# Start of a fused convolution and gated feed-forward kernel: the first input moved to other queues, and one mask cleared by another engine

## The chip, the cores and the metric

The kernel runs on one core of a Trainium2 chip. The metric is the device time of one execution in microseconds (us); lower is better. A core has five engines that run their own instruction streams: PE (TensorE, matrix products), DVE (VectorE), ACT (ScalarE), POOL (GpSimd) and SP (SyncE, which here only issues transfers). Transfers (DMAs) can be issued from SP, ACT and POOL, and all of them are moved by the same 16 DMA engines. Only a DMA that POOL issues changes the type on the way (float32 in memory to float16 on the chip); one from SP or ACT copies bytes.

## The reference

The input x is 8 sequences of 4096 tokens with 192 channels. A causal convolution over 7 tokens comes first, with one set of softmaxed weights per head (8 heads of 24 channels); after it a gated feed-forward layer.

```python
w = softmax(weight, axis=-1)                       # weight is [8 heads, 7 taps]
x_pad = concatenate([zeros(B, 6, D), x], axis=1)
out[b, s, h, g] = sum_k w[h, k] * x_pad[b, s + k, h, g]
t = out.reshape(B * S, D)                          # 32768 x 192
y = (maximum(t @ w_gate, 0) * (t @ w_val)) @ w_out # 192 -> 1536 -> 192
```

## The kernel before, in words

Two sequences are worked on at a time, as two "streams" (`st` 0 and 1, batch entries 0 and 4 at the start). They lie side by side in the partitions: 64 channels of stream 0 in partitions 0 to 63, the same channels of stream 1 in partitions 64 to 127. The work is cut into 16 units of 1024 tokens (`NUNIT`), each of two windows of 512 tokens. For each unit, `gate_val` multiplies the convolved input `xc` by `Wg` and `Wv` (PE, L505), ACT takes the positive part (L516), DVE multiplies the two (L517), and `project` multiplies by `Wo` (PE, L539, or L559 for the first unit). From unit 2 on the convolution itself is done by ACT, DVE and POOL beside the products. Units 0 and 1 are convolved on PE, with banded matrices: for unit 0 `conv_dense` (L333) multiplies 110 tokens of x by a 110 x 104 band per head.

The order on every engine is the order in which the program is written (`manual_schedule`). Everything that the change touches lies before the first product. Three things must be there before the first matmul of L333:

- The band matrices. `wr` (the weights) comes by SP (L104). DVE takes the maximum (`mx`, L214), ACT the exponential (`ex`, L217), DVE the sum, its reciprocal and `over` (L224). A matmul (L235) spreads them over 112 rows, DVE makes `diag` (L245), 14 matmuls with `places` (L255) spread that over the band, and DVE copies the first band out of PSUM (L288, `fill_band(0, [0, 1, 2], ...)`). `places`, `same` and `over` are made from `spaced`, a mask that is cleared (L129) and then gets its ones from POOL's `affine_select` (L131). ACT's first instruction is the load of its function table (L148), which comes with a small throwaway activation, `spare`.
- Stream 0's x. The first window is cut into five token steps of 104 tokens (`jj` 0 to 4). SP brings steps 1 to 4 in float32 into `stage`, an area in the tile `prods` (L125), and ACT casts them to float16 into `xts[0]`, the tile `x_h` (L279). Step 0 of both streams needs zeros ahead of the sequence: DVE clears the place (L140), SP brings it (L141), DVE casts it (L294).
- Stream 1's x, steps 1 to 4: POOL brings it, cast on the way, straight into `x_h` (L130).

For the first 64 channels L333 takes steps 1 to 4 of stream 0 first (16 matmuls), then steps 1 to 4 of stream 1 (16), then step 0 of both (8); the other two channel blocks of 64 follow with 40 matmuls each. Until then PE runs products of constants (`warm_up`, L157): seven at the start, one after L235, two after L255.

POOL's queue at the start is: clear `spaced` (L129), issue stream 1's x (L130), `affine_select` (L131), and then the issues of the weight slices `Wg` and `Wv` (L173) and of the next x (L90). DVE copies the first weight slice to the other 64 partitions (L180) before the first product with it.

Of the kernel before, what the change touches and what calls it, by code (L numbers as in the profile page):

```python
# [15 lines left out]
def kernel(  # L16
# [12 lines left out]
    nc = tc.nc  # L29

    B, S, D = x.shape
# [3 lines left out]
    PAD = KW - 1  # L35
    NB = B // 2
# [5 lines left out]
    SUB = 112  # L42
# [4 lines left out]
    GSUB = 5  # L47
    DSUB = 104
# [49 lines left out]
    xts = {}  # L98
    ROWS0 = DSUB + PAD
# [7 lines left out]
    def stage(p0, rows, st, n_st, jj, n):  # L107
        at = room[p0 : p0 + rows, 0, 0, 0:1]
        dims = [[D * GSUB, n_st], [D, n], [1, D]]
        return bass.AP(  # L110
            tensor=at.tensor,
            offset=at.offset + D * (GSUB * st + jj),
            ap=[at.ap[0]] + [d for d in dims if d[1] > 1],
        )

    xts[0] = xpool.tile([128, GSUB, 2, D], F16, name="x_h")

    def body(st):
        return bass.AP(
            tensor=x.tensor,  # L120
            offset=x.offset + (NB * st * S + DSUB - PAD) * D,
            ap=[[D, SUB], [DSUB * D, GSUB - 1], [1, D]],
        )

    nc.sync.dma_start(out=stage(0, SUB, 0, 1, 1, GSUB - 1), in_=body(0))  # L125
    ones = const.tile([128, SUB], FP)
    nc.vector.memset(ones[:], 1.0)
    spaced = const.tile([SUB, KW, SEG + 2 * GAP], FP)
    nc.gpsimd.memset(spaced[:], 0.0)  # L129
    nc.gpsimd.dma_start(out=xts[0][0:SUB, 1:GSUB, 1, :], in_=body(1))  # L130
    nc.gpsimd.affine_select(  # L131
        out=spaced[:, :, GAP : GAP + SEG],
        in_=ones[0:SUB, 0 : KW * SEG].rearrange("p (k s) -> p k s", k=KW),
# [8 lines left out]
        out=stage(PAD, DSUB, 0, 2, 0, 1),  # L142
        in_=bass.AP(
            tensor=x.tensor, offset=x.offset, ap=[[D, DSUB], [NB * S * D, 2], [1, D]]
        ),
# [53 lines left out]
    def summed(out, step, n, at):  # L199
# [15 lines left out]
        out=mx[:], in_=wr[:], axis=mybir.AxisListType.X, op=ALU.max, negate=True  # L215
# [9 lines left out]
        out=over[:],  # L225
# [10 lines left out]
        out=spread[0:SUB, 0, 0:H],  # L236
# [7 lines left out]
    with nc.allow_low_precision("products with one and zero"):  # L244
        nc.vector.tensor_tensor(  # L245
            out=diag[:],
# [6 lines left out]
    for a in range(2):  # L253
        for b in range(NSEG):
            nc.tensor.matmul(  # L255
                out=(bps, spread)[a][:, a, HB * SEG * b : HB * SEG * (b + 1)],
# [12 lines left out]
    for h in range(H):  # L269
        r = G * h  # L270
        while r < G * (h + 1):
            c, n = r // 64, min(64 - r % 64, G * (h + 1) - r)
            nc.sync.dma_start(
                out=tap[r % 64 : r % 64 + n, c, :],
                in_=taps[h : h + 1, :].unsqueeze(1).to_broadcast([1, n, KW]),
            )
            r += n

    nc.scalar.copy(out=xts[0][0:ROWS0, 1:GSUB, 0, :], in_=stage(0, ROWS0, 0, 1, 1, GSUB - 1))  # L279
    bands = {}  # L280

    def fill_band(a, heads, copy):
# [431 lines left out]
```

## Time and profile before

| what | value |
|---|---|
| median of 3 runs | 768.64 us (768.06 to 768.94) |
| span of the profiled execution, first to last instruction | 767.4 us |
| median less that span | 1.24 us |
| PE busy | 761.4 us, 99% of the span |
| DVE, ACT, POOL busy | 692.2, 601.7, 369.9 us |
| granted TensorE clock | 1.000 |

The profile shows one execution. Its own time has no row beside its span; the 1.24 us by which the median of the runs is longer is what lies around the span. Busy shares are averages over the whole span: PE at 99% is busy from about 6.5 us to the end, and what it lacks is in the first 6.5 us. Times in a timeline are counted from the start of the span. In a row of a timeline the first number is the start, the second the duration (of a group, from its first start to its last end), then engine, line, operation and operands; a bracket at the end gives the idle time before it and what ended it. "SPq", "ACTq" and POOL's DMA rows are the issuing of a transfer and not the transfer.

### The profile page before, as it was taken

How to read it: one execution, taken by the hardware profiler on the slowest of the kernel's cores; microseconds unless marked ns; L12 is line 12 of the kernel's file. 1: busy time of each engine (PE TensorE's matmuls, PEld its weight loads, DVE VectorE, ACT ScalarE, POOL GpSimd, SP SyncE). 2: the span in 40 equal slices, each digit the busy share in tenths (PEclk: the TensorE clock that was granted, in tenths of full speed). 3: DMA queues.
4: the chain of work that ended last, by engine and by line, in shares of the span. 5: the costliest groups of instructions: out<-in, count | busy, mean ns of one | idle time of the engine just before them, and what ended most of it. 6: DMA issues, size and time to landing. Idle time of an engine off the chain costs nothing.

```text
span 767.4 us, 24881 instructions
## 1 busy us (share of the span) xinstructions
PE 761.4 (99%) x10842; PEld 502.1 (65%) x10842; DVE 692.2 (90%) x745; ACT 601.7 (78%) x736; POOL 369.9 (48%) x212
## 2 busy tenths in 40 slices
PE   9999999999999999999999999999999999999997
PEld 4495674946649476584855848567494674947657
DVE  7999999999999999999999999999999999995590
ACT  6797887878888788888878878788787887874671
POOL 8608648093570926619165290843809355080000
PEclk9999999999999999999999999999999999999999
DMA  8956727180462705428064271722719131200202
GB/s 121 138 97 118 91 90 88 54 122 6 100 78 69 107 23 98 59 85 94 26 112 43 85 91 44 109 28 89 89 50 110 21 95 37 65 21 23 63 2 85
DMA packets 131827, 56.13 MB, mean 73 GB/s; under 512 B 96757, under 2 KB 131717, under 8 KB 131717
## 3 DMA queue, kind: packets, MB, share of 16 engines
q1 hardware_dynamic: 90805, 38.85, 24.9%
q0 software_dynamic: 40768, 15.59, 18.8%
q8 instruction: 85, 1.39, 0.8%
q14 instruction: 25, 0.20, 0.1%
q10 hardware_dynamic: 144, 0.10, 0.0%
HBM read 31.68 MB, written 25.17 MB: 74 GB/s over the span
## 4 chain that ended last, share of the span: by engine, by line
PE 99%; DMA 1%; issue 0%; DVE 0%; POOL 0%; POOLq 0%
PE ps L505 65%; PE ps L539 31%; PE ps L559 2%; DMA x_h<-in_x_dram 1%; PE ps L333 0%; PE ps L358 0%; DVE acc L576 0%; POOL spaced L129 0%; POOLq L698 0%
## 5 line engine op out<-in xcount | busy, mean ns | idle before, releaser
L517 DVE TENSOR_TENSOR hT<-gr,ps 128x1024 f16<-128x1024 f16 (+1 forms) x386 | 469.0, 1216 | 36.9 <-ACT gr L516 9.9
L516 ACT ACTIVATE gr<-ps 128x1024 f16<-128x1024 f32 (+1 forms) x386 | 393.3, 1020 | 101.9 <-PE ps L505 100.1
L458 POOL TENSOR_TENSOR prods<-prods 128x1344 f32<-128x1344 f32 x70 | 212.5, 3035 | 309.8 <-DVE prods L454 306.4
L505 PE MATMUL ps<-xc,Wg 64*128 64x512 f16 x2304 | 311.9, 376 | 0.0
L505 PE MATMUL ps<-xc,Wv 64*128 64x512 f16 x2304 | 311.8, 376 | 0.0
L539 PEld LDWEIGHTS <-hT 64*128 64x128 f16 x5760 | 238.0, 94 | 3.6
L539 PE MATMUL ps<-Wo,hT 64*128 64x192 f16 x5760 | 240.1, 243 | 0.0
L505 PEld LDWEIGHTS <-Wv 64*128 64x128 f16 x2304 | 129.6, 94 | 118.7 <-DVE hT L517 0.3
L505 PEld LDWEIGHTS <-Wg 64*128 64x128 f16 x2304 | 112.2, 94 | 132.5 <-issue 0.5
L481 DVE SCALAR_TENSOR_TENSOR acc<-x_r,tap,acc 128x576 f32<-128x576 f16 x210 | 154.3, 815 | 1.6 <-DMA x_r<-x_p 1.6
L452 ACT ACTIVATE prods<-x_r,tap 128x448 f32<-128x448 f16 x222 | 130.4, 664 | 0.0
L576 ACT COPY out_s<-ps 128x768 f32<-128x768 f32 (+1 forms) x64 | 46.2, 722 | 53.9 <-PE ps L539 44.0
L414 POOL DMA_DIRECT2D x_e<-in_x_dram x56 | 45.2, 818 | 3.3 <-POOL x_p L433 3.3
L433 POOL COPY x_p<-x_e 128x1728 f16<-128x1728 f16 x28 | 44.8, 1627 | 1.5 <-DMA x_e<-in_x_dram 1.5
L458 POOL TENSOR_TENSOR xc<-prods 128x1344 f16<-128x1344 f32 x14 | 42.4, 3026 | 1.1
L481 DVE SCALAR_TENSOR_TENSOR xc<-x_r,tap,acc 128x576 f16<-128x576 f16 x42 | 31.8, 816 | 0.0
L469 ACT ACTIVATE acc<-x_r,tap 128x576 f32<-128x576 f16 x42 | 29.4, 768 | 0.0
L454 DVE TENSOR_SCALAR prods<-x_r,tap 128x448 f32<-128x448 f16 x72 | 27.4, 452 | 0.0
L576 DVE COPY out_s<-ps 128x384 f32<-128x384 f32 x14 | 7.8, 556 | 14.8 <-ACT out_s L576 14.8
L559 PE MATMUL ps<-Wo,hT 128*128 128x192 f16 x192 | 16.2, 246 | 0.0
L559 PEld LDWEIGHTS <-hT 128*128 128x128 f16 x192 | 15.9, 98 | 0.0
L576 DVE COPY acc<-ps 128x192 f32<-128x192 f32 x1 | 0.4, 358 | 14.2 <-PE ps L539 14.2
(52 smaller groups left out, 62.6 us busy)
## 6 DMA issues: line engine op xcount, KB each, us to landing
out_dram<-out_s SPq DMA_DIRECT2D x62, 384.0 KB
x_e<-in_x_dram POOLq DMA_DIRECT2D x34, 192.0 KB, 6.2
x_e<-in_x_dram POOLq DMA_DIRECT2D x22, 240.0 KB, 5.0
x_r<-x_p SPq DMA_TRANSPOSE x126
Wo<-in_moe_w_out_dram POOLq DMA_DIRECT2D x1, 576.0 KB
x_h<-in_x_dram POOLq DMA_DIRECT2D x2, 240.0 KB, 7.3
x_h<-in_x_dram POOLq DMA_DIRECT2D x2, 210.0 KB, 4.7
x_h<-in_x_dram POOLq DMA_DIRECT2D x2, 192.0 KB, 7.7
```

The costliest lines, as they stand in the source:

```text
L414: nc.gpsimd.dma_start(out=xe[:, j : j + n, st, :, :].rearrange("p j c r -> p j (c r)"), in_=bass.AP(tensor=x.tensor, offset=x.offset + (b ...
L433: nc.gpsimd.tensor_copy(out=xp[:, :, :, st, :], in_=xe[:, :, st, :, :])
L452: engine.activation(out=out, in_=in_, func=ACTF.Copy, scale=scale)
L458: nc.gpsimd.tensor_tensor(out=pr[:, 0] if k < KW - 1 else xc[u][:, :, LDVE:UNIT], in0=pr[:, 0], in1=pr[:, k], op=ALU.add,)
L469: nc.scalar.activation(out=accs[u][:, c, :], in_=shifted(u, c, 0, 0), func=ACTF.Copy, scale=tap[:, c, 0:1],)
L481: nc.vector.scalar_tensor_tensor(out=xc[u][:, c, 0:LDVE] if k == KW - 1 else acc[:, c, :], in0=shifted(u, c, k, 0), scalar=tap[:, c, k : k ...
L505: nc.tensor.matmul(out=pss[i][:, st, :], lhsT=W[64 * st : 64 * st + 64, c, 128 * f : 128 * (f + 1)], rhs=xcb[64 * st : 64 * st + 64, c, WI ...
L516: nc.scalar.activation(out=gr[:, sts], in_=pss[0][:, sts], func=ACTF.Relu)
L517: nc.vector.tensor_tensor(out=h[:, f, sts], in0=gr[:, sts], in1=pss[1][:, sts], op=ALU.mult)
L539: mm = nc.tensor.matmul(out=outs[q], lhsT=h[64 * r : 64 * r + 64, f, st, 128 * q : 128 * (q + 1)], rhs=Wo[64 * r : 64 * r + 64, f, :], sta ...
L559: nc.tensor.matmul(out=outs[q], lhsT=h[:, f, st, 128 * q : 128 * (q + 1)], rhs=Wo[:, f, :], start=(f == 0), stop=(f == NFF - 1),)
L576: one(out=dst[:, step * j : step * j + step], in_=src[:, step * j : step * j + step])
```

## The change

Three edits, all ahead of the first product.

- POOL's first instruction becomes the issue of stream 1's x. It stood behind the clearing of `spaced`, which DVE does now, second in its queue, between `ones` and the clearing of the place for step 0.
- Stream 0's x, steps 1 to 4, is brought in two transfers: steps 1 and 2 from ACT's queue, steps 3 and 4 from SP's. Each has half the bytes.
- ACT casts the two halves with two instructions instead of one.

```diff
-    def body(st):
+    def body(st, jj, n):
         return bass.AP(
             tensor=x.tensor,
-            offset=x.offset + (NB * st * S + DSUB - PAD) * D,
-            ap=[[D, SUB], [DSUB * D, GSUB - 1], [1, D]],
+            offset=x.offset + (NB * st * S + DSUB * jj - PAD) * D,
+            ap=[[D, SUB], [DSUB * D, n], [1, D]],
         )
 
-    nc.sync.dma_start(out=stage(0, SUB, 0, 1, 1, GSUB - 1), in_=body(0))
+    nc.gpsimd.dma_start(out=xts[0][0:SUB, 1:GSUB, 1, :], in_=body(1, 1, GSUB - 1))
+    nc.scalar.dma_start(out=stage(0, SUB, 0, 1, 1, 2), in_=body(0, 1, 2))
+    nc.sync.dma_start(out=stage(0, SUB, 0, 1, 3, 2), in_=body(0, 3, 2))
     ones = const.tile([128, SUB], FP)
     nc.vector.memset(ones[:], 1.0)
     spaced = const.tile([SUB, KW, SEG + 2 * GAP], FP)
-    nc.gpsimd.memset(spaced[:], 0.0)
-    nc.gpsimd.dma_start(out=xts[0][0:SUB, 1:GSUB, 1, :], in_=body(1))
+    nc.vector.memset(spaced[:], 0.0)
     nc.gpsimd.affine_select(
...
-    nc.scalar.copy(out=xts[0][0:ROWS0, 1:GSUB, 0, :], in_=stage(0, ROWS0, 0, 1, 1, GSUB - 1))
+    for jj in (1, 3):
+        nc.scalar.copy(
+            out=xts[0][0:ROWS0, jj : jj + 2, 0, :], in_=stage(0, ROWS0, 0, 1, jj, 2)
+        )
```

In the built program each engine's list keeps its order but for these places: POOL begins with the issue of stream 1's x; DVE has the clearing of `spaced` second; ACT begins with the issue of its half, and the load of its function table (L148) comes behind that; SP has the same number of transfers, the second one of half the size. PE's list is the same.

## The prediction

> **What bounds the kernel now.** I read the page's busy shares first, then the chain of waits for the first 9 us, then the timeline of those 9 us, then the row of transfers that resemble the moved one.
>
> ```profile
> PE 761.4 (99%) x10842; PEld 502.1 (65%) x10842; DVE 692.2 (90%) x745; ACT 601.7 (78%) x736; POOL 369.9 (48%) x212
> ```
>
> PE is the bound: it lacks 6 us of the span. After 6.55 the chain of waits holds nothing but PE, so an edit at the start is worth exactly the time by which PE's unbroken run begins earlier or later. The chain up to there:
>
> ```profile
> 0.82 0.33 POOL spaced L129
> 1.16 0.28 issue
> 1.43 5.08 DMA x_h<-in_x_dram
> 6.51 0.04 issue
> 6.55 1.60 PE ps L333 x103
> 8.15 6.71 PE ps L505 x60
> ```
>
> Stream 1's x is what arrives last: POOL clears the mask (0.33), idles 0.28, issues at 1.43, and 5.08 later the data is there. What is next behind it is in the timeline:
>
> ```profile
> 0.82 1.28 ACT L148 ACT_TABLE_LOAD   x1 [0.82 <-PEq L698]
> 0.83 0.40 SPq L104 DMA_DIRECT2D wr<-in_weight_dram  x1
> 0.92 0.15 DVE L127 MEMSET ones<- 128x112 f32 x1 [0.92 <-PEq L698]
> 1.09 0.38 DVE L140 MEMSET prods<- 32x384 f32 x1
> 1.29 0.34 SPq L125 DMA_DIRECT2D prods<-in_x_dram  x1
> 1.68 0.46 SPq L141 DMA_DIRECT2D prods<-in_x_dram  x1
> 2.19 0.15 DVE L214 TENSOR_REDUCE mx<-wr 8x1 f32<-8x7 f32 x1 [0.46 <-DMA wr<-in_weight_dram]
> 2.37 0.39 ACT L217 ACTIVATE ex<-wr,mx 8x112 f32<-8x112 f32 x1
> 4.86 0.51 DVE L288 CAST band<-ps 128x336 f16<-128x336 f32 x1 [0.45 <-PE ps L255]
> 5.05 0.83 ACT L279 CAST x_h<-prods 110x768 f16<-110x768 f32 x1 [1.53 <-DMA prods<-in_x_dram]
> 5.93 2.22 PE L333 MATMUL ps<-band,x_h 110*32 110x104 f16 x120 [0.64 <-ACT x_h L279]
> 6.55 1.45 PEld L333 LDWEIGHTS <-x_h 110*32 110x32 f16 x104 [0.23 <-DMA x_h<-in_x_dram]
> ```
>
> Three arrivals in a row: the first band at 5.37 (4.86 + 0.51), stream 0's x cast at 5.88 (5.05 + 0.83), stream 1's x at 6.51. PE does stream 0's 16 matmuls from 5.93 to about 6.24 (their weight loads are 0.02 apart, so 0.31 for 16), and then waits until 6.55. Take the last arrival away and the next stands 0.3 behind it; the third 0.5 behind that.
>
> **The change part by part, as a sum over the three arrivals.**
>
> Stream 1's x. The issue loses the 0.33 of clearing ahead of it. Whether the 0.28 of idling goes too, the trace does not show: SP's first issue begins at 0.83 without a gap, which gives an issue at 0.82; if the gap belongs to every first issue it is 1.10. I take 0.95, nearer to SP's row. The 5.08 to landing I keep, because it is mostly the transfer's own:
>
> ```profile
> x_e<-in_x_dram POOLq DMA_DIRECT2D x22, 240.0 KB, 5.0
> ```
>
> Transfers of its kind, some of them with the DMA engines free at the time, need 5.0. So it lands at 6.03 (5.90 to 6.18) instead of 6.51, and PE can use it 0.04 later, at 6.07 (5.94 to 6.22).
>
> Stream 0's x. ACT issues its half at 0.82 instead of SP at 1.29, SP the other half at 1.29. The whole transfer needed 3.76 from issue to cast (1.29 to 5.05); half of it needs no more, so the halves land by 4.58 and 5.05 at the latest. A cast of 768 elements took 0.83 and one of 448 0.53 (L288 on ACT), so 384 take 0.46: the second half is cast by 5.51 at the latest, against 5.88. The extra cast costs 0.10 of ACT, beside the wait for data that ACT has anyway (1.53 before L279).
>
> The band. Here is the price. ACT's issue stands ahead of its table load, behind which `spare`, `ex` and the whole band chain are queued, and SP's tap transfers and the matmul of L235 wait for that chain. At the end of the trace there is one issue by ACT:
>
> ```profile
> 763.44 0.39 ACTq L577 DMA_DIRECT2D out_dram<-acc  x1
> ```
>
> SP's are 0.34 to 0.46. With 0.39 the table load ends at 2.49 instead of 2.10, `spare` (0.20) at 2.71, and `ex` starts at 2.76 instead of 2.37. Before, it waited for `mx` (ready 2.34) and `spare` (2.32) at once, so it has no slack, and the links to the band (sum, reciprocal, `over`, L235, `diag`, L255, copy) follow each other with gaps under 0.2. So the band comes at 5.76 instead of 5.37. The bounds are 0 (if the issue runs beside the load) and 0.46, SP's longest.
>
> The mask. DVE does 280 elements in about 0.31 (between 112 in 0.15 and 384 in 0.38), ready at 1.40. POOL comes to `affine_select` 0.33 to 0.61 earlier than 2.38, at 1.77 or later, so it waits for nothing; `over` needs it at about 3.6. On DVE the mask pushes `prods`, `places` and `ex`'s clearing 0.31 later, to about 2.05, still ahead of `mx`, which waits for `wr` until 2.19: nothing. But the clearing of `prods` ends at 1.78, so SP's step 0 (L141) is issued at 1.98, 0.3 later. With its old 4.09 it lands at 6.07 at the latest and is cast by 6.43, when PE has just finished stream 1's 16 matmuls (6.43): free, barely; it also has less ahead of it in SP's queue (half of L125). If that cover goes it costs up to 0.1, because band 3 and the weight copies stand behind the cast on DVE.
>
> POOL's other issues (`Wg`, `Wv`, next x) move 0.3 to 0.6 earlier with the first, so the weights, which DVE waited for until 6.91, come ahead of the need, and PE's steps after 8.15 move as a block.
>
> Sum: stream 0 can start when the band is there, 5.76 + 0.05 = 5.81; its 16 matmuls end at 6.12; stream 1 is there at 6.07. PE goes on at 6.12 instead of 6.55: 0.4 (0.33 to 0.43 over the bounds of the issue). The span becomes 767.0, and with the 1.24 around it the median 768.64 becomes 768.2.
>
> At one place a rule lowers that. In the window 3.2 to 3.4 the trace has 95 packets of the hardware queue and none of POOL's; POOL's began at 3.9, and from 4.4 to 4.6 there were 37 and 41. Moved earlier, POOL's packets meet more of SP's. The Trainium skill ("DMA: Bandwidth & Descriptors", Queues, rings and completion order) says that each DMA engine takes turns between its queues packet by packet; the window from 4.4 to 4.6 agrees. By that rule stream 1's x would land later than 6.03 by about the 0.2 that a share of the remaining packets takes (my estimate), and the gain would be 0.3 instead of 0.4.
>
> **The rivals.**
>
> No gain: POOL's first issue has a start of its own, or its transfer waits for SP's packets, and stream 1's x still lands at about 6.5. For: packets of POOL came only 2.5 after its issue, while for `x_e` (issue at 19.59) it was 1.6, so 0.9 of the 5.08 may be a fixed start. Against: 5.0 is the usual time. Time 768.6.
>
> More gain: ACT's issue does not hold up the table load. Then stream 0 starts at 5.51 + 0.05 and stream 1's x sets the time, at 5.94: 0.6, time 768.0.
>
> A late table: ACT's first issue costs more than SP's. PE starts stream 1 at 5.42 + d + 0.31, with d the delay of the table, so the change loses only if d is over 0.82. POOL's issue took 0.88, but ACT's and SP's were half of it. With d = 1.2 the time is 769.0.
>
> The other side, a slow PE: the seven constant products at the start end at 3.69, and L235 follows at 3.62 without a gap. With `ex` 0.39 later L235 starts at 4.01, and PE idles about 0.3. The first 512-column products are 0.425 apart (1.25, 1.67, 2.10, 2.53); the half-array pairs of L505 later are 0.215 apart, and the change of rate falls between 3.4 and 4.0, just where the new gap comes. If the gap puts the full rate off, all of L333 runs at half of it: 1.6 more for the 104 matmuls, 0.3 for stream 0's, 0.2 for L255, less 0.4: +1.7, 770.3. It takes the full rate to come after about 9.8; if it comes at 7, the loss is about 0.8 and the net +0.4. Against it: the work on PE is the same, and the gap of 0.64 ahead of 5.93 did not slow what follows and now shrinks to about 0.1. The Trainium skill ("TensorE: Matmul & The Clock Gate", Part 1) has the rule behind it: the PE clock is doubled only after a busy window of about 3.4 us, and the windows run freely. The profile's granted clock is 1.00 in all of these windows, so it cannot show this; the spacing of the matmuls can.
>
> **How the numbers follow.** Forecast 0.55; more gain 0.08; no gain 0.15; late table 0.08; slow PE 0.10; 0.04 is left for a gain that nothing in the profile shows. About 0.2% (1.5 us) is what a measurement of this kernel can tell from no change, and all cases but slow PE and the remainder lie within it, with 0.01 of the late table beyond: faster 0.04, same 0.85, slower 0.11. The range goes from the better case (768.0) to the late table (769.0), widened at each end by most of the 0.44 between the ends and the middle of the runs: 767.6 to 769.3.
>
> **What would show it.** Right: POOL's issue at 0.8 to 1.1, `x_h` landing near 6.0, ACT's table load at about 1.2 and `ex` at 2.76, the first band's copy ending at 5.76, L333's first matmul at 5.8 released by DVE's band and not by ACT's cast, and the unbroken run of PE from about 6.1. Wrong: `ex` still at 2.4 (more gain), `x_h` at 6.5 (no gain), 512-column products 0.43 apart after 4.0 or L333 taking over 2.5 (slow PE), or a chain of waits that leaves PE after 9 us.

## The result

The changed kernel is slower: 770.37 us in the median of 9 runs (769.49 to 771.00) against 768.54 us of the kernel before (9 runs, 767.70 to 768.94). The ratio is 1.0020, with an interval of 1.0012 to 1.0029. The forecast was 768.2 with a range of 767.6 to 769.3. In two further sessions, each on one chip, the ratio was 1.0025 (1.0015 to 1.0035) and 1.0015 (1.0006 to 1.0024).

The profiled execution of the changed kernel has a span of 768.2 us. Its chain of waits for the first 12 us no longer contains the landing of stream 1's x; it runs from ACT's issue through the band matrices (start, duration, engine and operation):

```profile
0.83 0.40 ACTq L126
...
2.75 0.29 ACT ex L218
...
4.07 0.51 PE ps L236 x2
4.58 0.54 PE ps L158
5.12 0.75 PE ps L256 x14
5.87 0.53 PE ps L158 x2
6.40 3.01 PE ps L337 x100
```

L337 is L333 of before. The chain begins to count it a little after its start: all 120 of its matmuls take 3.08 us (in the timeline below), 0.026 each, where the last 103 of before took 1.60, 0.0155 each. From then on PE is busy without a break in both kernels, so the 1.26 us by which it enters the products later (9.41 against 8.15) stay to the end of PE's work, at 763.06 before (754.81 + 8.25) and 764.33 after (759.79 + 4.54):

```profile
754.81 8.25 PE L539 MATMUL ps<-Wo,hT 64*128 64x192 f16 x196
759.79 4.54 PE L543 MATMUL ps<-Wo,hT 64*128 64x192 f16 x106
```

In the 20 profiles of this case PE ends 754.8 to 755.2 us behind the end of L333, wherever that lies. The spans of these two executions differ by 0.8 only. Behind PE's end, the last of the output landed after 3.0 us before and after 2.0 in the changed kernel, which is scatter (2.0 in 17 of the 20 profiles), and from that landing to the end of the span it took 1.3 before and 1.8 after, which is not; "The end of the program" below comes back to it.

What lies around the span was taken as 1.24 us ahead of the prediction. That was the median of the runs less the span of another execution. Where time and span of one execution are on record, the difference is 1.65 to 3.47 us over 153 executions of the kernel before (median 1.74) and 1.69 to 2.74 over 30 of the changed kernel (median 1.99). So one execution's time says little about a change of 1 us, and the span says more.

The timeline of the changed kernel's profile shows why PE enters the products later:

```profile
0.83 0.40 ACTq L126 DMA_DIRECT2D prods<-in_x_dram  x1
0.86 2.83 PE L158 MATMUL ps<-const-bfloat16-1.0 128*128 128x512 bf16 x7 [0.86 <-PEq L702]
1.26 1.28 ACT L149 ACT_TABLE_LOAD   x1 [1.26 <-PEq L702]
1.40 0.88 POOL L125 DMA_DIRECT2D x_h<-in_x_dram  x1 [0.87 <-POOLq L702]
2.66 0.37 ACT L218 ACTIVATE ex<-wr,mx 8x112 f32<-8x112 f32 x1
3.71 0.91 ACT L281 CAST x_h<-prods 110x384 f16<-110x384 f32 x2
4.07 0.51 PE L236 MATMUL ps<-over,ex 8*112 8x8 f32 x2 [0.38 <-DVE same L202]
4.51 0.61 PE L158 MATMUL ps<-const-bfloat16-1.0 128*128 128x512 bf16 x1
5.53 0.51 DVE L292 CAST band<-ps 128x336 f16<-128x336 f32 x1 [0.63 <-PE ps L256]
6.33 3.08 PE L337 MATMUL ps<-band,x_h 110*32 110x104 f16 x120
9.34 0.50 PE L509 MATMUL ps<-xc,Wg 64*128 64x512 f16 x2
9.68 0.38 PE L509 MATMUL ps<-xc,Wv 64*128 64x512 f16 x2
```

Three things are to be seen. POOL's issue did not move: it begins at 1.40 instead of 1.43, with 0.87 of idling ahead of it. The table load stands behind ACT's issue, the exponential comes at 2.66 instead of 2.37, and PE idles 0.38 ahead of L236. And the single 512-column product that follows takes 0.61; in the profile of before it took 0.39:

```profile
4.01 0.39 PE L157 MATMUL ps<-const-bfloat16-1.0 128*128 128x512 bf16 x1
```

This product is the gauge for the rest: 0.61 is PE at half rate, 0.39 at full rate. (Half, because such products start 0.425 apart in the first group and the pairs of L505 later 0.215 apart; a single duration and the pace of L333 change by less.) In the changed kernel the full rate comes only between 9.34 (0.50) and 9.68 (0.38); before, it came by 4.01. The granted clock column stays at 1.00 all the while and shows nothing of it.

### The profile page after: what moved, and what is told of

Same layout as the page of the kernel before. It is cut to its first block, busy times and chain, and to the rows that moved or that the text cites. A ratio compares the mean times of both kernels' runs of the same rounds, so it can differ in the third digit from the quotient of the medians.

```text
span 768.2 us, 24882 instructions
## 1 busy us (share of the span) xinstructions
PE 763.1 (99%) x10842; PEld 508.7 (66%) x10842; DVE 692.9 (90%) x746; ACT 601.2 (78%) x737; POOL 369.8 (48%) x211
## 3 DMA queue, kind: packets, MB, share of 16 engines
q8 instruction: 84, 1.38, 0.8%
## 4 chain that ended last, share of the span: by engine, by line
PE 99%; ACT 0%; DVE 0%; issue 0%; ACTq 0%; DVEq 0%
PE ps L509 65%; PE ps L543 31%; PE ps L563 2%; PE ps L337 1%; PE ps L362 0%; PE ps L158 0%; ACT L149 0%; PE ps L256 0%; PE ps L236 0%; DVE over L225 0%; ACTq L126 0%; DVE acc L580 0%; ACT ex L218 0%; ACT spare L149 0%; DVE sm L222 0%
## 5 line engine op out<-in xcount | busy, mean ns | idle before, releaser
L509 PEld LDWEIGHTS <-Wv 64*128 64x128 f16 x2304 | 131.6, 94 | 116.9 <-DVE hT L521 0.3
L509 PEld LDWEIGHTS <-Wg 64*128 64x128 f16 x2304 | 115.2, 94 | 129.3 <-issue 0.5
```

The costliest lines, as they stand in the source:

```text
L509: nc.tensor.matmul(out=pss[i][:, st, :], lhsT=W[64 * st : 64 * st + 64, c, 128 * f : 128 * (f + 1)], rhs=xcb[64 * st : 64 * st + 64, c, WI ...
```

## The experiments

Each time below is a median, beside that of the kernel before on the same chip; the ratio of the two has a 95% interval. "Rate at" is where the profile of that kernel changes from half to full rate, read from the 512-column products and the pace of L333 (about 0.025 a matmul at half rate, 0.0155 at full).

**Which part costs.** The split of stream 0's x alone, and POOL's part alone (issue first, mask on DVE):

```diff
+    nc.scalar.dma_start(out=stage(0, SUB, 0, 1, 1, 2), in_=body(0, 1, 2))      # split alone
+    nc.sync.dma_start(out=stage(0, SUB, 0, 1, 3, 2), in_=body(0, 3, 2))
-    nc.sync.dma_start(out=stage(0, SUB, 0, 1, 1, GSUB - 1), in_=body(0))
...
+    nc.gpsimd.dma_start(out=xts[0][0:SUB, 1:GSUB, 1, :], in_=body(1))          # POOL's part alone
...
-    nc.gpsimd.memset(spaced[:], 0.0)
-    nc.gpsimd.dma_start(out=xts[0][0:SUB, 1:GSUB, 1, :], in_=body(1))
+    nc.vector.memset(spaced[:], 0.0)
```

> The kernel before with the split of stream 0's x alone (half from ACT, half from SP, two casts); POOL's order and the mask as before. ACT's issue delays the table load and with it the exponential by 0.3. Theory A: the whole loss is here, 769.9 to 770.7, with L337 at half rate. Rival (the loss comes from POOL's and DVE's part): 768.3 to 768.8.

> The kernel before with POOL's part alone: the issue of stream 1's x first on POOL, the mask cleared by DVE; stream 0's x in one transfer from SP. Theory A (ACT's issue is what costs, and POOL's first issue begins at about 1.40 whatever stands ahead of it): the same as before, 768.2 to 768.8, x landing at 6.5 to 6.6, first PE product of L333 at 5.9. Rival (the later zero of step 0 or the mask on DVE cost something): 769 or more. Rival (POOL's issue does move here): 768.1 and an issue before 1.2.

The split: 770.16 against 768.76, ratio 1.0016 (1.0007 to 1.0025), nearly the whole loss, with the idle 0.39 on PE and the rate at about 8.9. Stream 1's x landed 4.9 us after its issue there, no later than before (5.1). POOL's part: 768.26, ratio 0.9991 (0.9982 to 0.9999). A repeat of POOL's part gave 768.74 against 768.32, 1.0001 (0.9990 to 1.0011), so neither a gain nor a loss is shown.

> POOL's part of the change alone, a second time. If it is a gain: 0.998 to 0.9995 of the kernel before. If the first session was scatter: 0.9995 to 1.0005. POOL's issue at 1.40 in both cases, so nothing of the forecast's earlier landing is expected.

Four lines of the first of the two profiles:

```profile
1.41 0.88 POOL L125 DMA_DIRECT2D x_h<-in_x_dram  x1 [0.87 <-POOLq L698]
4.09 0.61 PE L157 MATMUL ps<-const-bfloat16-1.0 128*128 128x512 bf16 x1
5.25 0.66 PE L157 MATMUL ps<-const-bfloat16-1.0 128*128 128x512 bf16 x2
5.88 1.96 PE L333 MATMUL ps<-band,x_h 110*32 110x104 f16 x120
```

POOL's first issue stays at 1.41 with nothing ahead of it. And PE is at half rate at 4.09 although nothing on PE's side differs from the kernel before: the rate changed at about 5.6 in this execution, and the time was good all the same.

**Does the idle time of PE do it?** One more constant product in the changed kernel closes the gap ahead of L236; one fewer opens a gap of 0.36 in the kernel before; and without the whole first group PE idles from the start to 3.64.

```diff
-    warm_up(512, 512, 512, 512, 512, 512, 128)
+    warm_up(512, 512, 512, 512, 512, 512, 512, 128)   # changed kernel, filled
+    warm_up(512, 512, 512, 512, 512, 128)             # kernel before, with a gap
...
-    warm_up(512, 512, 512, 512, 512, 512, 128)        # kernel before, no first group
```

> The changed kernel with one more 512-column constant product in the first warm-up group, so that PE is busy until about 4.1 us instead of 3.69, when the matmul of L236 starts at 4.07. Theory A (the idle 0.38 us of PE ahead of L236 puts the full rate off, and half-rate products up to 9.4 are the loss): full rate comes at about 4 again, the 120 matmuls of L337 take about 2.2 us instead of 3.1, PE's unbroken run starts where stream 1's x lands (6.6, as before), and the time is that of the kernel before, 768.2 to 768.8. Theory B (the loss is the later band chain and the queues themselves, the rate is an effect of the profile): nothing changes, 770.0 to 770.8. Theory C (the rate changes at random times in each execution, whatever PE did before): the spread stays and the middle lies anywhere between 768.5 and 770.4.

> The kernel before with one 512-column constant product fewer in the first warm-up group: nothing else is moved, PE just idles about 0.36 us from 3.26 to 3.62. Theory A (the idle time ahead of L235 puts the full rate off): L333 takes about 3 us, the time rises by 1.2 to 2.0 to 769.8 to 770.6. Theory B (it was the band chain and the queues): 768.3 to 768.8, no change. Theory C (random): no change of the middle beyond 0.3.

> The kernel before without the first group of seven constant products: PE idles until L235 at 3.62 instead of being busy from 0.86. Windows theory: a spoiled window costs the same whether 0.4 or 2.8 us in it are idle, and the full rate comes 3.4 to 6.8 after the first steady work; the loss is bounded by half rate for all of L333 (0.8 of PE's start, the rest being hidden by the wait for stream 1's x) and a part of the first products: 769.3 to 771. Rival (the rate depends on the amount of idle time): eight times the idle time of the kernel with one product fewer, and some 3 to 5 us, 772 or more.

Filled: 769.02 against 768.76, 1.0004 (0.9995 to 1.0012), rate at about 4.3, a little over the 768.2 to 768.8 that was expected. Its profile, an execution of 769.25 us, has no idle time ahead of L236 but a wait of L337 for stream 1's x:

```profile
4.51 0.39 PE L158 MATMUL ps<-const-bfloat16-1.0 128*128 128x512 bf16 x1
6.88 1.55 PE L337 MATMUL ps<-band,x_h 110*32 110x104 f16 x104 [0.43 <-DMA x_h<-in_x_dram]
```

With the gap: 769.31 against 768.76, 1.0005 (0.9996 to 1.0013), below the 769.8 to 770.6 of theory A. The profile has the rate at about 9.5:

```profile
3.62 0.51 PE L235 MATMUL ps<-over,ex 8*112 8x8 f32 x2 [0.36 <-ACT taps L267]
5.88 3.08 PE L333 MATMUL ps<-band,x_h 110*32 110x104 f16 x120
8.89 0.61 PE L505 MATMUL ps<-xc,Wg 64*128 64x512 f16 x2
```

Without the group: 769.29 against 768.28, 1.0006 (0.9997 to 1.0014). By these times neither of the two is told apart from no loss; the spans further down do tell them apart, with a loss that is smaller than the change's. It hardly grows with the idle time (0.36 or 2.8 us). In these two kernels the band is on time, L333 starts at 5.9, and at half rate it runs through the time in which it would have waited for stream 1's x. In the profile with the gap the first product starts at 8.89 against 8.09, 0.8 later and not 1.3.

**Is the place of the rate's change fixed?** The kernel before and the changed kernel, once more:

> The kernel before once more, for a second profile of the same program. If the place of the window differs from execution to execution, the change of rate (512-column products 0.61 long before it, 0.39 after it, in the first 10 us) need not fall at 3.4 to 4.0 again but anywhere from 3.6 to 10.4, and the time goes with it: about 767.8 with an early one, 769 to 770 with one after 7. If it is fixed, it is at 3.4 to 4.0 again.

> The changed kernel once more, on the chip of the three below. The theory by now (windows): the rate of PE is raised at the end of a time window of about 3.4 us whose place differs from execution to execution, if PE had little idle time in it; the idle 0.38 us ahead of L236 together with the tiny products of L236 (0.45) spoils every window that holds them, so the full rate comes at 7 to 10.5 instead of 3.6 to 7. Expected: 770.0 to 770.8, as before, and in the profile L337 partly or wholly at half rate. Rival (a draw of that day): within 0.5 of the kernel before.

The second profile of the kernel before, an execution of 770.85 us with a span of 767.8:

```profile
0.86 2.83 PE L157 MATMUL ps<-const-bfloat16-1.0 128*128 128x512 bf16 x7 [0.86 <-PEq L698]
3.62 0.54 PE L235 MATMUL ps<-over,ex 8*112 8x8 f32 x2
4.09 0.61 PE L157 MATMUL ps<-const-bfloat16-1.0 128*128 128x512 bf16 x1
5.91 3.29 PE L333 MATMUL ps<-band,x_h 110*32 110x104 f16 x120
9.53 0.59 PE L505 MATMUL ps<-xc,Wv 64*128 64x512 f16 x2
9.96 0.38 PE L505 MATMUL ps<-xc,Wg 64*128 64x512 f16 x2
```

The same program, the same starts up to 3.62, and the full rate comes between 9.53 and 9.96 instead of by 4.01. So the place differs between executions of one program. PE has no idle time at all in this profile from 0.86 to 9.53: a gap is not needed for a late rate. The changed kernel's second session gave 769.99 against 768.28, rate at about 9.3. In its third session the profile caught the opposite, an execution of 768.55 us:

```profile
4.07 0.33 PE L236 MATMUL ps<-over,ex 8*112 8x8 f32 x2 [0.38 <-DVE same L202]
4.33 0.39 PE L158 MATMUL ps<-const-bfloat16-1.0 128*128 128x512 bf16 x1
6.56 1.53 PE L337 MATMUL ps<-band,x_h 110*32 110x104 f16 x104 [0.28 <-DMA x_h<-in_x_dram]
8.03 0.39 PE L509 MATMUL ps<-xc,Wg 64*128 64x512 f16 x2
```

The late band costs nothing here: L337 waits for stream 1's x again, and the products start at 8.03, even a little ahead of the 8.09 of before. The change does its harm through how often the rate comes late. Of its 30 executions 27 took more than 769.3 us; of the 163 executions of the kernel before, 36 did.

**Is it the late band chain, without any transfer?** A useless activation ahead of the exponential in the kernel before, first of 224 and then of 448 elements (the edit shows 448):

```diff
     nc.scalar.activation(spare[:], ones[0:H, 0:1], ACTF.Exp)
+    idle = const.tile([128, 4 * SUB], FP)
+    nc.scalar.activation(idle[:].rearrange("p (a b) -> p a b", a=4), ones[:].unsqueeze(1).to_broadcast([128, 4, SUB]), ACTF.Exp)
```

> The kernel before with one useless activation of 224 elements on ACT ahead of the exponential, which makes it about 0.3 late; no transfer is moved or split, no queue changed. Windows theory: the late chain alone makes the idle time of PE ahead of L235 and the loss is that of the split: 769.8 to 770.6, L333 at half rate in most executions. Rival (the loss comes from transfers that contend, or from ACT's queue of transfers): 768.4 to 769.0, since the chain is covered by stream 1's x, which lands at 6.2 to 6.5 while the band would come at 5.7.

> The kernel before with a useless activation of 448 elements on ACT ahead of the exponential: with 224 elements the exponential came only 0.13 late and PE had no idle time ahead of L235 (3.69 to 3.73); now it should come about 0.3 late, as in the changed kernel, and PE should idle about 0.35 there. No transfer is touched. If the late chain with its idle PE is the cause, this alone gives the loss of the change: 769.8 to 770.5, with few executions below 769.2, and L333 at half rate in the profile. If the split transfer or ACT's queue is the cause: 768.3 to 769.1.

> The same late exponential with one more 512-column constant product in the first group, so that PE does not idle ahead of L235. If the idle PE is what costs: 768.4 to 769.0. If the lateness of the band by itself costs: as without the product, 769.8 to 770.5.

224 elements made the exponential only 0.13 late and left no gap on PE; 769.05 against 768.28, 1.0008 (0.9999 to 1.0017), undecided; in its one profile the rate came at about 9.5 all the same. 448 elements put it at 2.69, with 0.41 of idling ahead of L237 (L235 of before): 769.46 against 768.44, 1.0012 (1.0004 to 1.0021). With one more constant product the same late chain gives 768.35, 0.9999 (0.9990 to 1.0007). The two profiles, the late chain first and then the filled one:

```profile
4.10 0.51 PE L237 MATMUL ps<-over,ex 8*112 8x8 f32 x2 [0.41 <-DVE same L203]
4.54 0.61 PE L159 MATMUL ps<-const-bfloat16-1.0 128*128 128x512 bf16 x1
6.35 3.08 PE L335 MATMUL ps<-band,x_h 110*32 110x104 f16 x120
```

```profile
0.86 3.25 PE L159 MATMUL ps<-const-bfloat16-1.0 128*128 128x512 bf16 x8 [0.86 <-PEq L700]
4.38 0.39 PE L159 MATMUL ps<-const-bfloat16-1.0 128*128 128x512 bf16 x1
5.79 2.06 PE L335 MATMUL ps<-band,x_h 110*32 110x104 f16 x120
```

So the late chain with its idle PE costs by itself, without a transfer touched, and a filler takes the cost away though the exponential stays late (2.69 in both).

**ACT's issue behind the table load.**

```diff
-    nc.scalar.dma_start(out=stage(0, SUB, 0, 1, 1, 2), in_=body(0, 1, 2))
...
     nc.scalar.activation(spare[:], ones[0:H, 0:1], ACTF.Exp)
+    nc.scalar.dma_start(out=stage(0, SUB, 0, 1, 1, 2), in_=body(0, 1, 2))
```

> The changed kernel with ACT's issue of its half behind the table load and the small activation instead of ahead of them. The exponential is 0.05 to 0.4 late (it needs the issue too: about 0.4 after 2.3). If that issue delays it as much as before, the loss stays (770.0 to 770.8): then it is any issue on ACT ahead of the exponential, not the order against the table load, that costs. If the issue is beside the wait for the maximum, 768.3 to 768.8. From the row of 0.40 for the issue I expect the first: the exponential at 2.75, 770.2.

I had expected the issue to delay the exponential here too, and that was wrong. The issue ran beside the table load:

```profile
0.82 1.28 ACT L148 ACT_TABLE_LOAD   x1 [0.82 <-PEq L702]
1.11 0.39 ACTq L149 DMA_DIRECT2D prods<-in_x_dram  x1
2.38 0.39 ACT L218 ACTIVATE ex<-wr,mx 8x112 f32<-8x112 f32 x1
```

The time was 768.74 against 768.28, 1.0003 (0.9994 to 1.0012). Adding the 448 useless elements to this version brought the loss back in part:

> The changed kernel with ACT's issue behind the table load (768.74, the exponential on time), and in its place the 448 useless elements that make the exponential 0.3 late. Transfers as in the changed kernel, band chain as late as there, for another reason. If the late chain with the idle PE is the cause, the loss comes back: 769.5 to 770.5, and any excess over the late chain alone belongs to the split and POOL's part. If it was ACT's issue ahead of the table load in some other way, it stays at 768.7.

> The changed kernel, beside the late chain alone on the same chip. If the late chain with idle PE is all of it: within 0.3 of the late chain alone, both near 769.7. If the split adds a loss of its own: 0.5 or more above it, 770.0 to 770.5.

> The kernel before with the exponential 0.3 late (448 useless elements on ACT), no transfer moved, a second time: 769.2 to 769.8.

> The changed kernel with one more constant product, a second time: 768.4 to 769.0 if the idle PE is the cause. What is left above the kernel before (0.2 to 0.3 in the first session) is the part of the split: the wait for stream 1's x, which landed at 6.86 there.

All four on one chip against 768.75 us: the changed kernel 769.91, 1.0015 (1.0006 to 1.0024); the late chain alone 769.50, 1.0007 (0.9998 to 1.0015), which is 0.41 below it and so between the two expectations; the issue behind the table load with a late chain 769.74, 1.0008 (1.0000 to 1.0017); the changed kernel filled 769.55, 1.0009 (1.0000 to 1.0018). The filled kernel did worse than in its first session, and the issue behind the table load did too in a second one: 769.11 against 768.32, 1.0016 (1.0006 to 1.0025), where the late chain should have left nothing.

> The whole change but for the place of ACT's issue (behind the table load, exponential on time), a second time: if the late chain is all that costs, 0.999 to 1.0005 of the kernel before; if the split with POOL's part costs by itself through the later landing of stream 1's x, 1.0005 to 1.001.

So the late chain alone (0.12% and 0.07%) is about half of the change's loss (0.20%, 0.25%, 0.15%), and something else of the split is left, between nothing and 0.16% in four sessions of the versions without gap or without late chain (1.0004, 1.0009, 1.0003, 1.0016). A candidate is the landing of stream 1's x: in the five profiles of the changed kernel, filled or not, it took 5.1 to 5.5 us from its issue (mean 5.3), in the eleven profiles with stream 0's x in one transfer 4.5 to 5.1 (mean 4.8). Where the full rate is early, L337 waits for it: in both profiles of the filled kernel its last 104 matmuls start at 6.88 or 6.89, and the products at 8.36 and 8.39 (8.09 before). But with ACT's issue behind the table load the three landings were 4.7, 5.3 and 4.8, and the split alone, with nearly the whole loss, landed at 4.9. The split alone and the late chain alone even have the same times on PE (4.08 and 4.10 for the first matmul behind the gap, 6.34 and 6.35 for L333). So most of the rest is not at the start.

**The end of the program.** The last thing in the span is SP's list of waits, one for each semaphore in use, about 0.06 us apart, and then the engines stop together (L713, L709 in the kernel before). In the changed kernel the last output transfer has semaphore 107, the third of ten waits, and all that follow begin only when it has landed; in the kernel before it has semaphore 118, the last of the ten, and most of the list is done before the landing. The waits of SP from 760 us on for the last transfers show it, the changed kernel first, then POOL's part alone (us in total, times, longest):

```profile
SPq L713 <- DMA out_dram<-acc: 1.5, 1, 1.5
SPq L709 <- DMA out_dram<-acc: 1.0, 2, 0.7
```

From the last landing to the end of the span it took 1.79 to 1.87 us in all nine profiles with stream 0's x in two transfers (mean 1.83), and 1.31 to 1.46 in all eleven with one (mean 1.38). So the split costs 0.45 us (0.06%) there in every profile, whatever PE does at the start. That the transfer more shifts the numbers of the semaphores is what the two lists suggest; no run tests it apart from the split.

**What the spans show.** Every execution on record has its span, without the 1.65 to 3.47 us around it. In the profiles, the span was over 767.0 us in eight of the ten executions with the rate at 7.6 or later, and in three of the other ten, two of which have the split. Over all executions (spans of versions with the split hold the 0.45 too):

| kernel | executions with a span over 767.0 | median span | same chips, kernel before |
|---|---|---|---|
| changed kernel | 29 of 30 | 768.1 | 20 of 66 (two of three sessions) |
| split alone | 12 of 12 | 768.2 | 15 of 35 |
| issue behind the table load, late chain | 9 of 11 | 767.9 | 11 of 35 |
| late chain alone, 448 elements | 16 of 23 | 767.4 | 15 of 64 |
| late chain, filled | 2 of 11 | 766.4 | 4 of 29 |
| band on time, no first group | 9 of 11 | 767.6 | 9 of 31 |
| band on time, gap of 0.36 | 7 of 11 | 767.5 | 15 of 35 |
| changed kernel, filled | 15 of 22 | 767.25 | 26 of 70 |
| issue behind the table load | 11 of 23 | 766.9 | 14 of 54 |
| POOL's part alone | 3 of 22 | 766.35 | 20 of 58 |

The median span of the kernel before is 766.2 to 766.6 on each of these chips. So the gap with the band on time costs 0.9 and 1.2 us of the median span, the late chain with its gap 0.7 and 1.05, and the change 1.2 and 1.6 in its two later sessions. The filler brings the changed kernel down to 0.5 and 0.7 over the kernel before, which is little more than the 0.45 at the end of the program; and 0.45 and the late chain together make 1.15 to 1.5, about the whole change.

**A filler further on.** POOL's part alone, with 384 more columns of constant products behind L255, for the idle time ahead of L333:

```diff
-    warm_up(512, 128)
+    warm_up(512, 512)
```

> POOL's part of the change alone (which gave 768.26), with 384 more columns of constant products behind L255, ahead of L333, where PE still idles 0.4 to 0.6. If that idle time also spoils windows, fewer executions are late: 767.7 to 768.2. If not, 768.2 to 768.5; at half rate the extra columns cost 0.3 where PE does not wait.

768.17 against 768.44, 0.9998 (0.9989 to 1.0006): not told apart from the kernel before. No version here beats it beyond the interval.

## Why the prediction was wrong, point by point

**The issue of stream 1's x.** Forecast 0.95, with bounds of 0.82 and 1.10; measured 1.40, and 1.41 with POOL's part alone. The 0.28 of idling was read as something that follows the clearing of the mask, or that belongs to every first issue and starts with it. POOL's issue comes at 1.39 to 1.44 in all 20 profiles, with the clearing ahead of it or with nothing: the clearing cost no time there. The gain of 0.33 to 0.61 at the head of the sum was 0.03. The rival "no gain" had this right.

**The landing.** Forecast 6.03; 1.40 plus 5.2 is 6.6. The 5.08 kept for it was a single draw from a spread of 4.5 to 5.5. The row of 5.0 that supported it had a neighbour on the same page that did not, a smaller transfer of the same tensor that needs longer:

```profile
x_e<-in_x_dram POOLq DMA_DIRECT2D x34, 192.0 KB, 6.2
```

**Stream 0's x.** Right in its direction: both halves were cast by 4.62 (forecast: 5.51 at the latest). It was not the arrival that decided.

**The band.** Forecast 0.39 late; the issue took 0.40 and the table load began 0.44 later, but the exponential was only 0.29 late, because it began 0.11 after the small activation had begun and not after its end. The copy of the band ended at 6.04 instead of the forecast 5.76, and this is not the chain's work but PE's: L256 and the product ahead of it ran at half rate. In the execution of 768.55 us, at full rate, it ended at 5.69.

**The mask and step 0.** The mask moved as worked out, the maximum stayed at its place (2.20), step 0 was issued at 1.79 instead of the 1.98 of the forecast.

**The slow PE.** This is the step that failed: the sum kept PE at the pace of the one profile, and the case in which a gap changes that pace got a chance of 0.10 and no place in the sum. That rival decided, with its place (ahead of L236) and its idle time (0.38, forecast about 0.3). I took the one profile of the kernel before, where the rate rose by 4.01, as the property of the program, and asked what would put it off; I also held that the gap of 0.64 ahead of 5.93 had shown itself harmless, when in that execution the rate had already risen. The runs show the place of the rise to differ between executions, and the gap to move the odds. Over the profiles that were taken: of nine with at least 0.35 us of idling ahead of the matmul of L235, eight had the rate at 7.6 us or later; of eleven without it, nine had it before 6. The spread of the three runs known at the time, 768.06 to 768.94, was a hint that executions of this program differ in something, though not in what, since the time around the span varies by more. The Trainium skill ("TensorE: Matmul & The Clock Gate", Part 1) has the rule: the doubled clock needs a busy window of about 3.4 us, and the window runs freely and does not start with the kernel. The second profile of the kernel before agrees in that the place of the rise is not tied to the start, with 9.53 to 9.96 against 4.01 in the first. It does not agree that 3.4 us of busy PE are enough: by the profile PE was busy from 0.86 to 9.53 without the rise. The measurement decides, and which work a window counts as busy is not settled: L235 itself, 0.5 us of 8-column products, was borne in nine of those eleven.

**The price of the slow PE was met by luck.** It was forecast as 770.3, and 770.37 was measured. But its sum has 1.6 for the 104 matmuls of L333, as if their pace were halved like that of the 512-column products; at 0.025 against 0.0155 it is 1.0. By the sum the products would have begun 1.7 later, at 9.85; they began at 9.41, 1.26 later. The 0.45 at the end of the program, which the sum did not have, make up for it.

**The end of the program.** The forecast said that an edit at the start is worth exactly the time by which PE's unbroken run begins earlier or later. For PE's end that is right to 0.4 us in 20 profiles. For the span it is not: this term was put at nothing, and it is 0.45.

**Why the price was more than half rate alone.** With the band on time, half rate costs 0.8 of the start of the products, because L333 then uses the time in which it would have waited for stream 1's x. With the band late as well, L337 starts at 6.33 and nothing covers it: 1.26. The forecast treated the 0.39 of the band as hidden behind the landing; it is hidden at full rate only.

## What to carry to other kernels

Where PE is kept busy with filler ahead of its first real work, the filler's length is tied to the chain that it covers: what makes that chain later, even by 0.3 us off the critical path, opens a gap, and here gaps of 0.36 to 0.41 us cost 0.7 to 1.05 us of the median span, by making a late rate more frequent. Look at a 512-column product after the gap and not at the granted clock, and take a second profile of the same program before reading a start-up from one. Compare spans where the time around them varies by more than the change, and look at the end of the span too when an edit adds a transfer: here one at the start made the last waits 0.45 us longer. A transfer issued ahead of ACT's table load put the load off by 0.44 us here, with an issue of 0.40; issued behind it, it ran beside the load.

## What the runs showed of the hardware that was not expected

- PE's rate doubled at 4.01 or earlier in one execution of the kernel before and between 9.53 and 9.96 in another, with the same starts up to 3.62 us and with PE busy throughout from 0.86 to 9.53.
- POOL's first transfer is issued at 1.42 to 1.44 us with a clearing of 0.33 ahead of it, and at 1.39 to 1.41 with nothing.
- SP's waits at the end of the program follow each other at about 0.06 us; with the last output transfer third in their list the span ended 1.79 to 1.87 us behind its landing, with it last 1.31 to 1.46.
- The time of an execution was 1.65 to 3.47 us longer than its span in the kernel before.
- ACT's issue of 0.40 ahead of the table load put the load at 1.26; behind the load in the program it ran at 1.11, during the load, and the exponential stayed at 2.38.
- The same transfer of 168 KB by POOL took from 4.5 to 5.5 us to land, from one profile to the next.
